# A two-part kernel of local attention and a state-space layer: parameter loads, tables, the layout of C, 128-row blocks and a softmax in two halves

## The chip, the cores and the metric

The kernel runs on one core of a Trainium2 chip. A core has several engines that work side by side, each through its own queue in order: TensorE (PE, with its weight loads shown as PEld), VectorE (DVE), ScalarE (ACT), GpSimd (POOL) and SyncE (SP), which here only issues transfers. An engine's queue that issues transfers is written with a q (SPq, ACTq, POOLq). The metric is the device time of one launch in microseconds (us). PE accumulates into PSUM banks; ACT and DVE copy the results out of them.

## The reference

Two independent layers, each on 2048 tokens of width 448, side by side in the output:

```python
# A: 16 heads of 28; every token attends to itself and 7 tokens at distances 2, 4, ... 14
q, k, v = split_heads(A_x @ A_wqkv)
logits = einsum("bhsd,bhswd->bhsw", q, k[idx]) * 28 ** -0.5      # idx = pos - 2 * arange(8), masked below 0
a = einsum("bhsw,bhswd->bhsd", softmax(logits), v[idx]) -> (2048, 448) @ A_wo
# B: diagonal complex state space, 448 states
Lam_bar = exp(exp(log_dt) * Lam);  B_bar = ((Lam_bar - 1) / Lam)[:, None] * Bmat
Bu = x @ B_bar.T;   h[t] = Lam_bar * h[t-1] + Bu[t]
b = 2 * real(h @ Cmat.T) + x * Dskip
out = concatenate([a, b], -1)                                    # bfloat16
```

## The kernel before

Part A keeps 16 consecutive tokens (j = 0 to 15) in each of 128 partitions. `g_xta` transposes x (xTA) on PE, `proj_j` projects one j (four matmuls of 448 columns) to k_s, q_s or v_s, and `halo` copies the last 14 token slots of a partition to the next partition by four transfers that POOL issues. `qk_unit` makes the logits of one distance w for half of the j (jh = 0 or 1): DVE multiplies q and k (L363), adds the products down from 28 to 7 rows in two steps (L365, L366), `fill` puts other PE work in between, and seven matmuls with the identity (L370) finish the sum, which ACT copies to L (L371). After all 16 units comes one softmax over L (L439 to L453). The attention stage takes four j at a time (jg): for each w DVE makes pv = attn x v (L487), PE transposes and sums pv over w in the banks of acc (L492), ACT copies acc to oT (L496), and `wo_tile` applies wo (L474) later, out of the list of work.

Part B works on chunks of T = 4 tokens: 512 chunks are columns, and 448 complex states are 7 blocks m of 128 rows (64 real, 64 imaginary). The parameters are loaded as 33 rows by twelve small transfers (L72 to L75), transposed by PE (L165) and turned into coefficients on DVE and ACT (L168 to L181); powers of Lam_bar (`s_pow`), gains (`s_gain`) and the matrices R (`s_R`) follow. Cosine and sine tables of 512 steps are made in four pieces q by `s_tab1` to `s_tab4` on ACT and DVE during the k projections, and spread to tab by twelve transfers on SP's queue (L268 to L270). C is laid out by POOL in copies (L126, L127) and transposed and scaled by `c_prep` during the q projections. `b_prep` transposes B to BT; `bu_tile(m, j)` multiplies it with x (L329) and adds R times the state before (L332). x and B have 448 columns, so that the last of four blocks uses 64 rows, 64 to 127 (`blk_rows`). `ssm_chunk_scan` runs the recurrence over the chunks on DVE for half of the blocks (HF), `fix_tile` adds its result to the other tokens (L392, L393), and `c_tile` makes outputs with C (L403) and the skip term (dgD, L407), again with 64 rows in the last block.

The order of all queues is the order of the program (`manual_schedule`). Work for PE waits in the list `work` with a cost in us for each item, and `fill(us)` takes items until that much is used up. Tiles with one tag share one place in memory: nat (the tables) and L do, C's layout (CC), BT and v_s do, and PSUM has four banks "mm" for projections and tiles, two "tp" for transposes, two "lg" for logits; acc later takes the place of the last four.

Of the kernel before, what the change touches and what calls it, by code (L numbers as in the profile page):

```python
# [14 lines left out]
J = 16  # L15
# [13 lines left out]
def kernel(  # L29
# [39 lines left out]
    rows = const.tile([33, 128], BF16, tag="rows")  # L69
    for r0, vec in ((18, B_log_dt), (7, B_Lambda_im), (0, B_Lambda_re)):  # L70
        for hf in range(2):
            nc.scalar.dma_start(rows[r0:r0 + 7, 64 * hf:64 * hf + 64], vec.rearrange("(m i) -> m i", i=64))  # L72
    for r0, vec in ((25, B_log_dt), (14, B_Lambda_im), (29, B_Dskip)):
        nc.scalar.dma_start(rows[r0:r0 + 3, :], vec[0:384].rearrange("(m i) -> m i", i=128))
        nc.scalar.dma_start(rows[r0 + 3:r0 + 4, :], vec[320:448].rearrange("(m i) -> m i", i=128))  # L75
# [17 lines left out]
    CC = keep.tile([128, 12800], BF16, tag="v", name="CC")  # L93
    Cn = CC[:, 0:3584].rearrange("p (k r n) -> p k r n", k=4, r=2)
    Cil = CC[:, 3584:10752].rearrange("p (s k m a i) -> p s k m a i", s=2, k=4, m=NM, a=2)
    nsn = CC[:, 10752:12800].rearrange("p (q c) -> p q c", q=4)
# [4 lines left out]
    nc.sync.dma_start(Bn[0:64], B_B_re.rearrange("(m i) n -> i m n", i=64))  # L101
    nc.sync.dma_start(Bn[64:128], B_B_im.rearrange("(m i) n -> i m n", i=64))
# [6 lines left out]
    load_w(2)  # L109

# [13 lines left out]
    for s_ in range(2):  # L124
        for ri in range(2):
            nc.gpsimd.tensor_copy(Cil[:, s_, 0:3, :, ri ^ s_, :], Cn[:, 0:3, ri].rearrange("p k (m i) -> p k m i", i=64))  # L126
            nc.gpsimd.tensor_copy(Cil[0:64, s_, 3, :, ri ^ s_, :], Cn[0:64, 3, ri].rearrange("p (m i) -> p m i", i=64))  # L127
# [18 lines left out]
    def halo(eng, dst):  # L146
        eng.dma_start(dst[1:65, 0:HALO], dst[0:64, J:JK])
        eng.dma_start(dst[65:113, 0:HALO], dst[64:112, J:JK])
        eng.dma_start(dst[112:128, 0:HALO], dst[111:127, J:JK])
        eng.dma_start(dst[0:1, 0:HALO], dst[0:1, J:JK])  # L150
# [12 lines left out]

    tpp = psum_t.tile([128, 4, 128], BF16, tag="tp", name="tpp")
    PE.transpose(tpp[:, 0, 0:33], rows[:], ident[0:33, 0:33])  # L165
    prm = const.tile([128, 33], F32, tag="prm")
    V.tensor_copy(prm[:], tpp[:, 0, 0:33])
    lre, lim, lima, lda, dsk = prm[:, 0:7], prm[:, 7:14], prm[:, 7:18], prm[:, 18:29], prm[:, 29:33]  # L168
    dt = pt_("dt", 11); ACT.activation(dt[:], lda, ACTF.Exp)
    are = tt(pt_("are"), dt[:, 0:7], lre, ALU.mult)  # L170
    th = tt(pt_("th", 11), dt, lima, ALU.mult)
    r = pt_("r"); ACT.activation(r[:], are[:], ACTF.Exp)
    rT = pt_("rT"); ACT.activation(rT[:], are[:], ACTF.Exp, scale=float(T))
    f = ts(pt_("f"), th[:, 0:7], 1.0 / (2 * PI), ALU.mult)
    fT = ts(pt_("fT", 4), th[:, 7:11], float(T) / (2 * PI), ALU.mult)
# [5 lines left out]
    ACT.activation(cs[:], af1[:], ACTF.Sin, bias=hpib[:], scale=-2 * PI * SHR)  # L181


    nat = keep.tile([128, 2, 4, NC], BF16, tag="L", name="nat")
    pw = const.tile([128, T - 1, 2, NM], F32, tag="pw")
# [4 lines left out]
    tabs = {}  # L190

    def s_tab1(q):
        c1 = slice(q, q + 1)
        yy = early.tile([128, NC], F32, tag="yy", name="yy")
        kM = early.tile([128, NC], F32, tag="kM", name="kM")
        nfr = early.tile([128, NC], F32, tag="nfr", name="nfr")
        tabs[q] = nfr
        ACT.activation(yy[:], iot[:], ACTF.Identity, scale=fT[:, c1])
        V.tensor_scalar(kM[:], iot[:], fT[:, c1], MAGIC, ALU.mult, ALU.add)
        V.scalar_tensor_tensor(nfr[:], kM[:], -MAGIC, yy[:], ALU.add, ALU.subtract)  # L200

    def s_tab2(q):
        ACT.activation(nat[:, 1, q, :], tabs[q][:], ACTF.Sin, scale=-2 * PI * SHR)

    def s_tab3(q):
        afr = early.tile([128, NC], F32, tag="afr", name="afr")
        ACT.activation(afr[:], tabs[q][:], ACTF.Abs)
        tabs[q] = afr

    def s_tab4(q):  # L210
        ACT.activation(nat[:, 0, q, :], tabs[q][:], ACTF.Sin, bias=hpib[:], scale=-2 * PI * SHR)
# [8 lines left out]

    gr = {}
# [20 lines left out]
    dgD = bk.tile([128, 4, 128], BF16, tag="dgD")  # L242

    def s_dgD():
        for blk in range(4):
            V.tensor_scalar(dgD[:, blk, :], ident[:], dsk[:, blk:blk + 1], None, ALU.mult)

    side = {}
    for q in range(4):
        for n, fn in enumerate((s_tab1, s_tab2, s_tab3, s_tab4)):  # L250
            side[4 * q + n] = [(fn, (q,))]
    side[2].append((s_pow, ()))
    side[6].append((s_gain, ()))
    side[10].append((s_dgD, ()))
    for jg in range(4):
        for kt in range(4):
            g_xta(jg, kt)
        for j in range(4 * jg, 4 * jg + 4):
            proj_j(1, k_s, HALO, j)
            for fn, args in side[j]:  # L260
                fn(*args)
    halo(nc.gpsimd, k_s)
    s_R()
    V.tensor_scalar(nsn[:], nat[:, 1], -1.0, None, ALU.mult)

    tab = bk.tile([128, 2, NM, NC], BF16, tag="tab")
    for dst, c, srcs in ((lo, 0, nat[:, 0]), (hi, 0, nat[:, 0]), (lo, 1, nsn), (hi, 1, nat[:, 1])):
        nc.sync.dma_start(tab[dst, c, 0:6:2, :], srcs[lo, 0:3, :])  # L268
        nc.sync.dma_start(tab[dst, c, 1:6:2, :], srcs[hi, 0:3, :])
        nc.sync.dma_start(tab[dst, c, 6, :], srcs[hi, 3, :])  # L270
# [3 lines left out]
    Cw = bk.tile([128, NM, D], BF16, tag="Cw")  # L274

    def c_prep(m):
        tps = []
        for s_ in range(2):
            tp = psum_t.tile([128, 512], BF16, tag="tp", name="tp")
            for dq in range(4):  # L280
                n = 64 if dq == 3 else 128
                PE.transpose(tp[:, 128 * dq:128 * dq + n], Cil[0:n, s_, dq, m].rearrange("p a i -> p (a i)"), ident[0:n, 0:n])
            tps.append(tp)
# [3 lines left out]


    for n, j in enumerate(list(range(8, 16)) + list(range(0, 8))):
        if n < NM:  # L290
            c_prep(n)
        proj_j(0, q_s, 0, j)
    early_ctx.close()
# [8 lines left out]

    BT = keep.tile([128, 4, NM, 128], BF16, tag="v", name="BT")

    def b_prep(m):
# [4 lines left out]
        ACT.copy(BT[:, :, m, :], tp[:])  # L310
    for m in range(NM):
        work.append((0.23, b_prep, (m,)))

    def blk_rows(blk):
        return slice(64, 128) if blk == 3 else slice(0, 128)

    late = {}
    bz = ctx.enter_context(tc.tile_pool(name="b_z", bufs=1, side="right"))

    def new_z():  # L320
        late["Z"] = bz.tile([128, NM, T, NC], BF16, tag="Z", name="Z")
        late["scr"] = bk.tile([128, NM, NC], BF16, tag="scr", name="scr")
    work.append((0, new_z, ()))

    def bu_tile(m, j):
        Z = late["Z"]
        ps = psum.tile([128, 512], F32, tag="mm", name="mm")
        for blk in range(4):
            PE.matmul(ps[:], BT[blk_rows(blk), blk, m, :], xT4[blk_rows(blk), blk, j, :],  # L329
# [4 lines left out]
    HF = (range(0, 4), range(4, 7))  # L334
    for ms in HF:
        for j in range(T):
            for m in ms:
                work.append((0.86 if j == 0 else 1.08, bu_tile, (m, j)))
# [4 lines left out]
    def v_halo():  # L343
        halo(nc.gpsimd, late["v"])

    def new_v():
        late["v"] = keep.tile([128, JK, DH, H], BF16, tag="v", name="v_s")
    work.append((0, new_v, ()))
    for j in range(J):
        work.append((0.76, v_tile, (j,)))  # L350
    work.append((0, v_halo, ()))


    L = keep.tile([128, W, JH], F32, tag="L", name="L")


    UNITS = [(w, 1) for w in range(5)] + [(w, 0) for w in range(5)] + [(w, jh) for w in range(5, 8) for jh in (1, 0)]

    def qk_unit(u, us):
        w, jh = UNITS[u]  # L360
        off = HALO - 2 * w
        pr = qkp.tile([128, DH, JH // 2], BF16, tag="prod", bufs=2, name="prod")
        V.tensor_tensor(pr.rearrange("p d (j h) -> p d j h", h=H), q_s[:, :, 8 * jh:8 * jh + 8, :],  # L363
                        k_s[:, off + 8 * jh:off + 8 * jh + 8].rearrange("p j d h -> p d j h"), ALU.mult)
        V.tensor_tensor(pr[:, 0:14, :], pr[:, 0:14, :], pr[:, 14:28, :], ALU.add)  # L365
        V.tensor_tensor(pr[:, 0:7, :], pr[:, 0:7, :], pr[:, 7:14, :], ALU.add)  # L366
        fill(us)
        lg = psum_l.tile([128, JH // 2], F32, tag="lg", name="lg")
        for d in range(7):
            PE.matmul(lg[:], ident[:], pr[:, d, :], start=(d == 0), stop=(d == 6))  # L370
        ACT.copy(L[:, w, 128 * jh:128 * jh + 128], lg[:])  # L371

    def ssm_chunk_scan(ms):
        Z, scr = late["Z"], late["scr"]
# [14 lines left out]
    def fix_tile(m, j):  # L389
        Z = late["Z"]  # L390
# [7 lines left out]
    def c_tile(j, ct):  # L398
        Z = late["Z"]
# [131 lines left out]
```

## Time and profile before

| | us |
|---|---|
| three runs | 228.36, 226.02, 223.96; median 226.02 |
| profiled execution | 225.31, its span 223.5 |
| PE busy (1376 matmuls) | 178.9 (80%) |
| PE weight loads | 106.2 (48%) |
| DVE busy | 158.1 (71%) |
| ACT busy | 101.3 (45%) |
| POOL busy | 15.1 (7%) |

The stages in the timeline of that execution: the first matmul of k at 13.94, of q at 40.2, the first transposes of B at 61.35, the first matmul of v at 102.65, the last c tile at 156, the first matmul of attention at 168.17, the last copy out of PSUM until 220.5. The span is the time between the first and the last instruction in the profile. In the page a slice is a fortieth of the span, its digit the tenth of it in which the engine was busy; PEclk is the clock granted to TensorE in tenths. In the timeline a line has start, duration, engine, line of the program, operation, tiles, shape and count, and in brackets the idle time before it with what ended it.

### The profile page before, as it was taken

The page shows a single profiled execution, that of the slowest core. Times are in us where ns is not written, and L with a number is a line of the kernel's source. Part 1 is how long each engine was busy: PE and PEld are TensorE (multiplying, and loading weights), DVE is VectorE, ACT ScalarE, POOL GpSimd, SP SyncE. Part 2 cuts the span into 40 slices and gives each one's busy share as a digit, 9 for nine tenths or more (in the row PEclk, how much of TensorE's full clock was granted, in tenths as well). Part 3 has the DMA queues.
Part 4 walks back from the last instruction along what each step waited for, and adds up shares of the span by engine and source line. Part 5 has one row for each costly group of instructions (what it writes and reads, how often), then busy time and mean ns, then how long its engine had stood idle before and what let it go on. Part 6 is the DMA issues. An engine that isn't in the chain of part 4 may idle for free. (4 is left out here: it accounts for less than half of the span.)

```text
span 223.5 us, 3466 instructions
## 1 busy us (share of the span) xinstructions
PE 178.9 (80%) x1376; PEld 106.2 (48%) x1380; DVE 158.1 (71%) x190; ACT 101.3 (45%) x187; POOL 15.1 (7%) x37
## 2 busy tenths in 40 slices
PE   0084679599979999999999799999009979797973
PEld 0052345355534333434544456555009968686851
DVE  0059676833936889799999999987399998584002
ACT  0265178746684445445789723333600022415151
POOL 4039000201000000000010200000000000000000
PEclk9999699979999999999999999999855969999998
DMA  6899970599600000000019421111002001111102
GB/s 189 253 246 185 190 149 19 125 198 186 96 0 0 3 0 0 0 0 3 0 31 191 67 66 62 63 53 62 30 0 76 0 3 43 44 41 43 42 26 97
DMA packets 19911, 16.10 MB, mean 72 GB/s; under 512 B 9624, under 2 KB 19128, under 8 KB 19640
## 3 DMA queue, kind: packets, MB, share of 16 engines
q1 hardware_dynamic: 19372, 12.65, 23.9%
q0 software_dynamic: 416, 3.24, 8.1%
q8 instruction: 10, 0.16, 0.3%
q14 instruction: 5, 0.04, 0.1%
q10 hardware_dynamic: 108, 0.01, 0.0%
HBM read 5.05 MB, written 3.67 MB: 39 GB/s over the span
## 5 line engine op out<-in xcount | busy, mean ns | idle before, releaser
L492 PE MATMUL acc<-ident,pv 128*112 128x128 bf16 x512 | 34.6, 233 | 16.0 <-DVE pv L487 11.6
L492 PEld LDWEIGHTS <-pv 128*112 128x112 bf16 x512 | 34.3, 143 | 18.3 <-DVE pv L487 12.0
L363 DVE TENSOR_TENSOR prod<-q_s,k_s 128x3584 bf16<-128x3584 bf16 x16 | 32.3, 2021 | 9.0 <-PE lg L370 7.8
L487 DVE TENSOR_TENSOR pv<-attn,v_s 128x1792 bf16<-128x1792 bf16 x32 | 32.8, 1085 | 4.6 <-PE acc L492 4.5
L329 PE MATMUL mm<-xT,BT 128*128 128x512 bf16 (+1 forms) x108 | 31.0, 381 | 0.2
L142 PEld LDWEIGHTS <-xTA 112*128 112x128 bf16 x192 | 19.0, 104 | 18.6 <-issue 3.2
L333 ACT CAST Z<-mm 128x512 bf16<-128x512 f32 x28 | 16.4, 586 | 19.9 <-PE mm L332 16.5
L403 PE MATMUL mm<-Cw,Z 128*128 128x448 bf16 x112 | 23.9, 353 | 0.0
L329 PEld LDWEIGHTS <-BT 128*128 128x128 bf16 x112 | 10.0, 97 | 18.0 <-issue 13.0
L479 ACT CAST ya<-mm 128x448 bf16<-128x448 f32 x14 | 7.5, 533 | 22.9 <-PE mm L474 19.9
L365 DVE TENSOR_TENSOR prod<-prod 128x1792 bf16<-128x1792 bf16 x16 | 17.5, 1092 | 0.5
L410 ACT CAST yo<-mm 128x448 bf16<-128x448 f32 x16 | 8.5, 532 | 20.0 <-PE mm L407 20.0
L496 ACT CAST oT<-acc 112x2048 bf16<-112x2048 f32 x4 | 7.5, 1866 | 21.7 <-PE acc L492 21.7
L474 PE MATMUL mm<-wo_p,oT 112*128 112x448 bf16 x64 | 14.9, 364 | 1.2 <-ACT oT L496 1.2
L142 PE MATMUL mm<-wk,xTA 112*128 112x448 bf16 x64 | 15.7, 403 | 0.0
L142 PE MATMUL mm<-wq,xTA 112*128 112x448 bf16 x64 | 14.4, 374 | 0.0
L403 PEld LDWEIGHTS <-Z 128*128 128x128 bf16 x112 | 10.0, 98 | 7.9
L144 ACT CAST k_s<-mm 128x448 bf16<-128x448 f32 x16 | 8.4, 525 | 9.7 <-PE mm L142 9.6
L136 PE MATMUL tp<-ident,xh 128*112 128x128 bf16 x64 | 6.4, 253 | 7.4 <-DVE xTA L137 7.4
L142 PE MATMUL mm<-wv,xTA 112*128 112x448 bf16 x64 | 12.3, 352 | 0.0
L477 DVE CAST ya<-mm 128x448 bf16<-128x448 f32 x2 | 1.2, 624 | 14.9 <-PE mm L474 14.9
L144 ACT CAST q_s<-mm 128x448 bf16<-128x448 f32 x16 | 8.5, 532 | 6.8 <-PE mm L142 6.8
(116 smaller groups left out, 229.5 us busy)
## 6 DMA issues: line engine op xcount, KB each, us to landing
xh<-in_A_x_dram SPq DMA_DIRECT2D x4, 448.0 KB, 3.4
out_dram<-yo SPq DMA_DIRECT2D x16, 112.0 KB, 1.7
out_dram<-ya SPq DMA_DIRECT2D x16, 112.0 KB, 1.7
tab<-nat SPq DMA_DIRECT2D x6, 192.0 KB, 11.5
k_s<-k_s POOLq DMA_DIRECT2D x1, 784.0 KB, 6.0
v_s<-v_s POOLq DMA_DIRECT2D x1, 784.0 KB, 5.9
k_s<-k_s POOLq DMA_DIRECT2D x1, 588.0 KB, 11.1
v_s<-v_s POOLq DMA_DIRECT2D x1, 588.0 KB, 9.3
```

Source lines behind the costliest of these rows:

```text
L142: PE.matmul(ps[:, 0:D], xTA[:, kt, j, :], w_of[t][:, kt, :], start=(kt == 0), stop=(kt == 3))
L144: ACT.copy(o_ap, ps[:, 0:D].rearrange("p (h d) -> p d h", h=H))
L329: PE.matmul(ps[:], BT[blk_rows(blk), blk, m, :], xT4[blk_rows(blk), blk, j, :], start=(blk == 0), stop=(blk == 3 and j == 0))
L333: ACT.copy(Z[:, m, j, :], ps[:])
L363: V.tensor_tensor(pr.rearrange("p d (j h) -> p d j h", h=H), q_s[:, :, 8 * jh:8 * jh + 8, :], k_s[:, off + 8 * jh:off + 8 * jh + 8].rearra ...
L365: V.tensor_tensor(pr[:, 0:14, :], pr[:, 0:14, :], pr[:, 14:28, :], ALU.add)
L403: PE.matmul(ps[:, 0:D], Z[:, m, j, cols], Cw[:, m, :], start=(m == 0), stop=False)
L410: ACT.copy(yo[:], ps[:, 0:D])
L474: PE.matmul(ps[:, 0:D], oT[:, kt, j, :], wo_p[:, kt, :], start=(kt == 0), stop=(kt == 3))
L479: ACT.copy(ya[:], ps[:, 0:D])
L487: V.tensor_tensor(pv[:], attn[:, w, JG * H * jg:JG * H * (jg + 1)].rearrange("p (j h) -> p j h", h=H) .unsqueeze(2).to_broadcast((128, JG, ...
L492: PE.matmul(acc[0:KT, kt, jj, :], pvf[:, jj, KT * kt:KT * (kt + 1)], ident[:], start=(w == 0 and jj == 0), stop=(w == W - 1 and jj == JG - 1))
```

## The change

- The parameters come in four loads, each vector twice side by side (128 columns for 7 blocks); four transposes make the columns, and the forms for 128-row blocks are put together by small DVE copies (`to_blocks`, for dsk and fT).
- PE runs 24 zero matmuls of 128 columns ahead of these transposes and 12 behind them (`idle`).
- The table steps keep their four pieces for the fraction (`s_yy`, `s_frac`), at other places of the k projections, but sin, the absolute value (now on DVE) and cos are each one operation on 2048 elements (`t_sin`, `t_cos`) in the q projections; the spread takes eight transfers, after the second last q projection. `s_R` is queued in the last k projection.
- C is laid out by twelve DVE copies (`c_side`) after the k projections, in three strips (re, im, re) of which `c_prep` takes two neighbours; `c_prep` comes with every second q projection.
- The fourth block of B and of the skip term has 128 rows, whose first 64 weights are zero.
- BT is prepared one m ahead of its bu tile. The units of jh = 1 come first, those of jh = 0 after the scans with one add less and 14 matmuls for the sum. The softmax runs by halves of j (`soft_max`, `soft_norm`), the attention takes jg = 2, 3, 0, 1, copies acc to oT in four pieces and runs wo directly after each jg.
- `halo`'s third transfer begins one partition later.

The diff, cut:

```diff
-    rows = const.tile([33, 128], BF16, tag="rows")
-    for r0, vec in ((18, B_log_dt), (7, B_Lambda_im), (0, B_Lambda_re)):
-        for hf in range(2):
-            nc.scalar.dma_start(rows[r0:r0 + 7, 64 * hf:64 * hf + 64], vec.rearrange("(m i) -> m i", i=64))
...
+    VECS = (B_log_dt, B_Lambda_re, B_Lambda_im, B_Dskip)
+    rows = const.tile([NM, len(VECS), 2, 64], BF16, tag="rows")
+    for n, vec in enumerate(VECS):
+        nc.scalar.dma_start(rows[:, n], vec.rearrange("(m o i) -> m o i", o=1, i=64).to_broadcast((NM, 2, 64)))
...
+    zero = const.tile([128, 128], BF16, tag="zero")
+    V.memset(zero[:], 0.0)
+    idle_ps = psum_l.tile([128, 128], F32, tag="lg", name="idle_ps")
+    def idle(n):
+        for _ in range(n):
+            PE.matmul(idle_ps[:], zero[:], zero[:], start=True, stop=True)
...
-            nc.gpsimd.tensor_copy(Cil[:, s_, 0:3, :, ri ^ s_, :], Cn[:, 0:3, ri].rearrange("p k (m i) -> p k m i", i=64))
-            nc.gpsimd.tensor_copy(Cil[0:64, s_, 3, :, ri ^ s_, :], Cn[0:64, 3, ri].rearrange("p (m i) -> p m i", i=64))
...
-        eng.dma_start(dst[112:128, 0:HALO], dst[111:127, J:JK])
+        eng.dma_start(dst[113:128, 0:HALO], dst[112:127, J:JK])
...
+    def to_blocks(dst, src):
+        V.tensor_copy(dst[lo, 0:4], src[lo, 0:7:2])
+        V.tensor_copy(dst[hi, 0:3], src[hi, 1:6:2])
+        V.tensor_copy(dst[hi, 3:4], src[hi, 6:7])
+    idle(24)
     tpp = psum_t.tile([128, 4, 128], BF16, tag="tp", name="tpp")
-    PE.transpose(tpp[:, 0, 0:33], rows[:], ident[0:33, 0:33])
+    for n in range(4):
+        PE.transpose(tpp[:, 0, 8 * n:8 * n + NM], rows[:, n].rearrange("m a i -> m (a i)"), ident[0:NM, 0:NM])
+    idle(12)
...
+    side = {2: [(s_pow, ())], 5: [(s_yy, (0,))], 6: [(s_gain, ()), (s_frac, (0,))], 8: [(s_yy, (1,))],
+            10: [(s_frac, (1,)), (s_dgD, ())], 11: [(s_yy, (2,))], 13: [(s_frac, (2,))], 14: [(s_yy, (3,))],
+            15: [(s_frac, (3,)), (s_R, ())]}
...
+    def c_side(k):
+        for s_, ri in enumerate((0, 1, 0)):
+            n = 64 if k == 3 else 128
+            V.tensor_copy(Cil[0:n, k, :, s_, :], Cn[0:n, k, ri].rearrange("p (m i) -> p m i", i=64))
+    c_side(0); c_side(1); c_side(2); c_side(3)
...
+    def t_sin():
+        ACT.activation(nat[:, 1], nfr[:], ACTF.Sin, scale=-2 * PI * SHR)
+        V.scalar_tensor_tensor(afr[:], nfr[:], -1.0, nfr[:], ALU.mult, ALU.max)
+    def t_cos():
+        ACT.activation(nat[:, 0], afr[:], ACTF.Sin, bias=hpib[:], scale=-2 * PI * SHR)
+        V.tensor_scalar(nsn[:], nat[:, 1], -1.0, None, ALU.mult)
+        for dst, c, srcs in ((lo, 1, nsn), (hi, 1, nat[:, 1]), (lo, 0, nat[:, 0]), (hi, 0, nat[:, 0])):
+            nc.sync.dma_start(tab[dst, c, 0:7:2, :], srcs[lo, 0:4, :])
+            nc.sync.dma_start(tab[dst, c, 1:6:2, :], srcs[hi, 0:3, :])
     for n, j in enumerate(list(range(8, 16)) + list(range(0, 8))):
-        if n < NM:
-            c_prep(n)
+        if n == 1:
+            t_sin()
+        if n % 2 == 1 and n < 14:
+            c_prep(n // 2)
         proj_j(0, q_s, 0, j)
+        if n == 14:
+            t_cos()
...
+    nc.gpsimd.memset(BT[lo, 3], 0.0)
...
-            PE.matmul(ps[:], BT[blk_rows(blk), blk, m, :], xT4[blk_rows(blk), blk, j, :],
+            PE.matmul(ps[:], BT[:, blk, m, :], xT4[:, blk, j, :],
...
+    bu = [[(0.86 if j == 0 else 1.08, bu_tile, (m, j)) for j in range(T) for m in ms] for ms in HF]
+    fix = [[(0.43, fix_tile, (m, j)) for j in range(T - 1) for m in ms] for ms in HF]
+    work += bu[0]
+    for w in range(4):
+        qk_unit(w, 1, 3.0, True)
+    fill(99)
+    work += bu[1]
+    for w in range(4, 6):
+        qk_unit(w, 1, 3.0, True)
     ssm_chunk_scan(HF[0])
+    fill(99)
     ssm_chunk_scan(HF[1])
+    late["v"] = keep.tile([128, JK, DH, H], BF16, tag="v", name="v_s")
+    work += [(0.76, v_tile, (j,)) for j in range(J)] + fix[0]
     fill(99)
+    halo(nc.gpsimd, late["v"])
+    work += fix[1][:6]
+    fill(99)
+    work += fix[1][6:] + [(1.55, c_tile, (j, ct)) for j in [T - 1] + list(range(T - 1)) for ct in range(4)]
+    qk_unit(6, 1, 1.5, True)
+    qk_unit(7, 1, 2.5, True)
+    soft_max(1)
+    qk_unit(0, 0, 2.5, False)
+    qk_unit(1, 0, 2.5, False)
+    soft_norm(1)
+    fill(3.0)
+    for w in range(2, 8):
+        qk_unit(w, 0, 2.3, False)
+    soft_max(0)
+    fill(99)
...
+    for jg in (2, 3, 0, 1):
...
+            if jg == 2 and w == 4:
+                soft_norm(0)
...
+        for jj in range(JG):
+            j = JG * jg + jj
+            if jg == 1 and jj % 2 == 1:
+                V.tensor_copy(oT[:, :, j, :], acc[0:KT, :, jj, :])
+            else:
+                ACT.copy(oT[:, :, j, :], acc[0:KT, :, jj, :])
+        for jj in range(JG):
+            wo_tile(JG * jg + jj, jg == 1)
```

`soft_max(jh)` masks with POOL, takes the maximum over w, subtracts it (DVE) and exponentiates (ACT) for 128 of the 256 columns of L; `soft_norm(jh)` adds up, inverts and multiplies to attn (DVE).

## The prediction, made before the result was known

> **What bounds the kernel now.** I read the page first: its slices of busy time and granted clock show which stage has which limit.
>
> ```profile
> span 223.5 us, 3466 instructions
> PE   0084679599979999999999799999009979797973
> DVE  0059676833936889799999999987399998584002
> PEclk9999699979999999999999999999855969999998
> ```
>
> A slice is 5.6 us. TensorE (PE) idles in slices 1 and 2, limps through 3 to 11, is full from 12 to 27, idles in 28 and 29 with the clock falling, then works on to the end. DVE is nearly full from 16 to 27 too, so in the middle two engines are close to binding at once. Next I read the timeline of the first 45 us.
>
> ```profile
> 7.61 0.26 ACTq L75 DMA_DIRECT2D rows<-in_B_Dskip_dram  x1
> 11.20 0.18 PE L165 MATMUL tpp<-ident,rows 33*128 33x33 bf16 x1 [11.20 <-DMA rows<-in_B_Dskip_dram]
> 13.94 4.78 PE L142 MATMUL mm<-wk,xTA 112*128 112x448 bf16 x16
> 18.76 3.49 DVE L156 TENSOR_TENSOR pw<-pw 128x7 f32<-128x7 f32 x1
> 20.93 1.30 POOL L126 COPY CC<-CC 128x1344 bf16<-128x1344 bf16 x1
> 24.36 1.01 PE L136 MATMUL tp<-ident,xh 128*112 128x128 bf16 x8 [5.19 <-DVE xTA L137]
> 36.25 3.32 PE L142 MATMUL mm<-wk,xTA 112*128 112x448 bf16 x16
> 39.73 2.96 DVE L239 TENSOR_TENSOR R<-II,cf 128x2688 bf16<-128x2688 bf16 x1
> ```
>
> Three readings. PE's queue starts with the transpose of the parameters, so everything waits for the twelfth small load (issued 7.61, there at 11.2), while x and wk have long landed. A DVE operation on 7 numbers takes 3.49 us while POOL lays out C (its neighbours take 0.16): DVE is held, the xTA copies behind it are late, and PE waits 5.19. Sixteen projection matmuls need 4.78 us at 14 us and 3.32 at 36; their weight loads stand 0.37 apart at first and 0.19 later, a half and a full clock. The timeline around 92 us shows one tile of the B stage.
>
> ```profile
> 91.33 0.39 PE L332 MATMUL mm<-Z,R 128*128 128x512 bf16 x1
> 91.56 1.13 PE L329 MATMUL mm<-xT,BT 128*128 128x512 bf16 x4
> 92.30 0.09 PEld L329 LDWEIGHTS <-BT 64*128 64x128 bf16 x1 [0.42 <-issue]
> 92.62 0.39 PE L332 MATMUL mm<-Z,R 128*128 128x512 bf16 x1
> ```
>
> From R matmul to R matmul are 1.29 us for five matmuls of 0.215: the 64-row weights are loaded late and cost 0.21. Last, the softmax.
>
> ```profile
> 164.63 2.29 DVE L453 TENSOR_TENSOR attn<-L,m 128x2048 bf16<-128x2048 f32 x1
> 168.17 10.19 PE L492 MATMUL acc<-ident,pv 128*112 128x128 bf16 x128 [11.64 <-DVE pv L487]
> 178.40 1.87 ACT L496 CAST oT<-acc 112x2048 bf16<-112x2048 f32 x1 [18.04 <-PE acc L492]
> ```
>
> PE does nothing for 11.64 us, then also waits for each of four 1.87 us copies. The chain of waits is the softmax, then the attention stage on PE to the end.
>
> **To the first k matmul (13.94 before).** Four loads replace twelve. The first six were issued by 3.1, the seventh only at 4.65, so the eight removed carry the lateness. Landing takes 3.4 us for an xh load and 5.1 for wk; four loads issued by 2.4 should be there between 4.2 and 6.3, I take 5.3. Four transposes take 0.4. DVE then has the old chain (11.42 to 12.66, 1.24 us) and six block copies of 0.16, less the 0.28 in which it waits for ACT anyway: 1.9 us ahead of the xTA copies. From the first of these to the first matmul are 1.28 (12.66 to 13.94): k starts at 8.9. The zero matmuls: 0.37 x 128/448 = 0.107 each at half clock; 24 end by 3.9, before the loads; 12 take 1.3, under DVE's 1.9. So they cost nothing; without that cover, 1.3. wk is there at 6.3. **-5.0 us.**
>
> At best the zero matmuls make k start warm. The trace went to full speed at 17.2, after 3.3 us of unbroken work; 24 of them are 2.6 us. I take half clock for the first part of k, 1.1 us, between 0 (warm) and 2.9 (16 x 0.18).
>
> [...]
>
> **k stage (13.94 to 39.6 before).** A warm group of four j is 4.61 us (31.64 to 36.25), 3.05 of it matmuls. Without POOL's copies the 5.19 stall goes, and with it the half clock at 24.3 to 27.4. What is late next is DVE's side work: powers 14 x 0.17 = 2.4, gain 1.9 + fraction 1.2 = 3.1, fraction + dgD 2.0, each against 3.05 of matmuls. Hidden, within 0.2. 3.05 + 3 x 4.61 + 1.1 = 18: k ends at 26.9. **-7.7 us.** The twelve ACT table steps of 512 leave this stage; ACT had room.
>
> **q stage (39.6 to 61.35 before): the loss.** The C layout moves into DVE's queue, behind the last fraction (waits for ACT's yy; done 1.3 after k ends), R (0.55 + 2.96) and ahead of all Cw. Twelve copies of 448 bf16: no such row. Below, DVE's smallest operation, 0.16; above, the xTA copy (512 from PSUM), 0.42. I take 0.25, nearer the small end since the 2048-element bf16 negation takes only 0.69: 3.0 us, between 1.9 and 5.0. PE transposes for c_prep(0) after one projection, and needs all twelve: it stands from 0.75 to 7.8 after k. Then afr (2048, four times 0.69 = 2.8) is ahead of the first Cw, and c_prep(1) waits 0.6 for that. PE's work: 16 x 0.755 + 7 x 0.95 = 18.7. Sum 18.7 + 7.05 + 0.6 = 26.3. After so long an idle time the clock halves, as at 44.4 to 47.9 (granted 0.51): 1.5. 27.8 against 21.75: **+6.0 us**; q ends at 54.7, called T.
>
> [...]
>
> **T to the first attention matmul (106.8 before).** PE's entry is later: on ACT the one cos (2048; as the exp of 2048, 1.91) stands ahead of the last q copy and of BT's copies, so the first bu tile starts at T+2.9. POOL's zeros for BT (896 elements; twice the 0.56 copy of 448) are under that.
> - bu: 7 x 4 x 0.215 + 21 x 5 x 0.215 = 28.6, where 34.5 stood (-5.9). If 128 rows don't cure the gap, 0.
> - preps 1.4, six logit groups of seven at 0.4, v 16 x 0.755: to T+47.5.
> - 21 fix tiles at ACT's pace 0.495 (the 18 copies in 8.91), three c tiles 7 x 0.19 + 4 x 0.056 = 1.55 each (before 1.73), two logit groups: to T+63.4. DVE has finished its eight products and both scans (14.6 + 11.3) by T+56 and waits.
> - The softmax's operations have half the columns. The trace has them whole: 1.23, 0.69, 0.43, 2.29 for the maximum and the difference, the reciprocal 1.75; a half costs about the next smaller one (128 elements: 0.29, between 0.16 for 7 and 0.43 for 256). L copy and POOL's memset 0.65, maximum 0.69 + 0.43 + 0.29 + 1.23 + gaps = 2.75; its exp is under the products. DVE: two products with one add (2.02 + 1.09 = 3.15), normalization (0.69 + 0.43 + 0.29 + 0.9 + 1.23 + gaps) 3.65, six products 18.9: with stalls of 0.1 on PE T+95.8. PE has 14-matmul groups of 0.8 and the last thirteen c tiles; it waits 3.5 for the first of these products and 2 to 4 at the end, when c tiles have run out. Then group 0.8, copy and memset 0.7, maximum 2.75, pv 1.09: T+101.2.
> Clock lost in these two waits: 1.0. 102.2 against 106.8: **-4.6 us.**
>
> L takes the slot of nat, and the table transfers (eight instead of twelve, the same bytes) now start only at T-0.2, behind the last cos; SP's queue holds nothing else until the first output. 1.79 MB at about 0.2 MB/us (53 to 55 us) land at T+10; L's first copy wants T+7.8. ACT stands still, but PE has four mm buffers, 4 us of tiles. Cost 0; every us past T+11.5 is on the path.
>
> **Attention to the end (55.3 before).** First group: seven pv 7.6, normalization of the other half 3.65 in DVE's queue, last matmuls 0.95: 12.2. This group is of the j whose logits came first, so that only one half of the softmax stands ahead of it. Then three times oT piece 0.6 + four wo 3.04 + 128 x 0.0565 = 10.87 (before 11.54), and 0.6 + 3.04 + ya 0.62 + 3.0 from the last copy to the end. 52.1: **-3.2 us.** wo_p's load is free to go before this stage. The halo's third piece no longer waits 10.9 for the second: nobody needed it.
>
> **Sum.** -5.0 - 7.7 + 6.0 - 4.6 - 3.2 = -14.5. The profiled execution had 225.3 (span 223.5); the median shown is 226.0. 225.3 - 14.5 = 210.8: **211 us.**
>
> **Rivals.**
> - *Slower: L's slot.* In the trace the same table transfers took from 37.3 to past 57, with single issues of 3.28 and landings of 11.5. Eight such issues and one landing end at T+37.5: ACT's first L copy holds all behind it for 26 us: 237. It decides against the change from T+26. Against: the slow ones ran beside k_s's halo, which is over by then.
> - *128 rows cure nothing.* 28 x 0.21 + 16 x 0.18 = 8.8 come back: 220. Against: matmuls with full rows stand 0.215 apart.
> - *The q stall is short.* Copies at 0.16 and a clock that stays up, k warm: 1.1 + 1.1 + 1.5 + 1.0 less: 206.
> - *The clock stays down* through k's start (1.8 more), twice as long after the q stall (1.5) and in the first attention group (16 x 0.107 = 1.7 per pv instead of 1.09 for the last three, 1.9): 216.
>
> **How the numbers follow.** Forecast (208 to 214) 0.48; shorter stall 0.16; clock 0.16; no cure 0.08; L's slot 0.06; nothing of these, another wait of 10 us or more, 0.06. Range 203 to 221. About 2% (221.5 and 230.5) is what a measurement of this kernel can tell from no change: faster 0.86, same 0.07, slower 0.07.
>
> **What would show it.** Right: tpp near 5.5; no 3.49 us power; PE idle about 7 us before the first Cil transpose; bu tiles of 1.08; an attention start with 4 us of idle in front. Wrong: ACT idle ahead of its first L copy with PE following; bu tiles still at 1.29; more than 10 us of PE idle in q.

## The result, and the profile after

The changed kernel takes 212.62 us (median of four runs, 210.73 to 212.74); the kernel before, beside it, 227.19 (223.96 to 228.39). The ratio is 0.943, with a 95% interval of 0.931 to 0.955. The profiled execution took 212.74, its span is 211.0. Forecast were 211 and a range of 203 to 221. Ratios, here and below, leave out executions that were over 1.5% slower than the fastest of their kernel.

The page of the changed kernel first, with slices of 5.3 us:

```profile
span 211.0 us, 3648 instructions
PE   5699952999789999999999949999428589898983
DVE  0569769613695998999996099998959999988013
PEclk9999996599979999999999999999955999999999
```

TensorE works from slice 1 on. Three holes are left: slices 5 and 6 (the q stage; the clock falls in 6 and 7), slice 23 (the first product behind the first half of the softmax) and 28 to 31 (the last logits and the wait ahead of the attention, the clock falling in 29 and 30). PEclk shows no half clock in the first slices; that k starts at half clock is read from the distances of its weight loads, 0.37 and then 0.19, as in the prediction. DVE's row has a hole in slice 22, where before it was nearly full. The timeline of the first 40 us:

```profile
4.91 0.18 PE L175 MATMUL tpp<-ident,rows 7*128 7x7 bf16 x1 [1.05 <-DMA rows<-in_B_Lambda_re_dram]
7.05 0.18 PE L175 MATMUL tpp<-ident,rows 7*128 7x7 bf16 x1 [0.52 <-DMA rows<-in_B_Dskip_dram]
10.61 4.09 PE L144 MATMUL mm<-wk,xTA 112*128 112x448 bf16 x16
15.99 3.32 PE L144 MATMUL mm<-wk,xTA 112*128 112x448 bf16 x16
33.23 3.59 DVE L270 COPY CB<-CB 128x448 bf16<-128x448 bf16 x12
33.96 0.29 PE L279 MATMUL tp<-ident,CB 128*128 128x128 bf16 x1 [4.52 <-DVE CB L270]
34.84 0.29 PE L279 MATMUL tp<-ident,CB 128*128 128x128 bf16 x1 [0.59 <-DVE CB L270]
36.74 2.27 DVE L290 SCALAR_TENSOR_TENSOR afr<-nfr 128x2048 f32<-128x2048 f32 x1
```

The last three parameter loads are there at 4.91, 6.34 and 7.05, one after another; the first is there by 3.67, when PE has finished its 24 zero matmuls (at 2.14 in e2, which has none). The k stage has no stall (the 3.49 us power and the 5.19 us wait are gone). In q, PE stands for 4.52 us and then three times for 0.59 behind DVE's copies of C. Two windows of the same stage (columns: stretch, its length, then busy time and count of PE, PEld, DVE, ACT and POOL, the granted clock, the DMA share, GB/s):

```profile
34.00:36.00 2.00, 0.82 (x3) 0.26 (x3) 2.00 (x8) 0.00 (x0) 0.00 (x0) 0.50 1.35 257
40.00:42.00 2.00, 2.00 (x12) 1.04 (x11) 0.28 (x1) 1.12 (x2) 0.00 (x0) 0.50 0.01 1
```

The clock is still 0.50 after the stall, when PE has no gap. By the windows around these it is a half from 32.9 to 43.15. The timeline of the B stage and of the end:

```profile
67.03 0.27 ACT L407 COPY L<-lg 128x128 f32<-128x128 f32 x1 [1.30 <-PE mm L349]
...
73.28 0.38 PE L349 MATMUL mm<-Z,R 128*128 128x512 bf16 x1
73.50 1.03 PE L346 MATMUL mm<-xT,BT 128*128 128x512 bf16 x4
74.36 0.38 PE L349 MATMUL mm<-Z,R 128*128 128x512 bf16 x1
...
121.05 0.69 DVE L420 TENSOR_TENSOR m<-L 128x512 f32<-128x512 f32 x1 [6.80 <-POOL L L417]
...
126.91 0.95 PE L406 MATMUL lg<-prod,ident 128*128 128x128 bf16 x14 [3.37 <-DVE prod L398]
...
158.83 6.46 PE L505 MATMUL acc<-ident,pv 128*112 128x128 bf16 x80 [4.38 <-DVE pv L498]
...
170.62 2.04 ACT L512 CAST oT<-acc 112x512 bf16<-112x512 f32 x4 [11.70 <-PE acc L505]
```

bu tiles are 1.08 apart (1.29 before). ACT waits 1.30 us ahead of its first L copy, and no PE row of this stretch shows a wait for it. DVE has nothing to do for 6.80 us ahead of the first half's softmax, and PE then waits 3.37 for the first product behind it (predicted 3.5). PE waits 4.38 ahead of the attention, 11.64 before, and then four copies of a quarter of acc take 2.04 us together.

### The profile page after: what moved, and what is told of

Same layout as the page of the kernel before. It is cut to its first block, busy times and chain, and to the rows that moved or that the text cites. A ratio compares the mean times of both kernels' runs of the same rounds, so it can differ in the third digit from the quotient of the medians.

```text
span 211.0 us, 3648 instructions
## 1 busy us (share of the span) xinstructions
PE 177.9 (84%) x1471; PEld 113.2 (54%) x1475; DVE 156.8 (74%) x214; ACT 99.1 (47%) x195; POOL 9.1 (4%) x33
## 3 DMA queue, kind: packets, MB, share of 16 engines
HBM read 5.05 MB, written 3.67 MB: 41 GB/s over the span
## 4 chain that ended last, share of the span: by engine, by line
PE 56%; DVE 10%; issue 3%; ACT 2%; POOL 0%; POOLq 0%; DVEq 0%
PE mm L346 12%; PE acc L505 12%; PE mm L382 8%; PE mm L485 6%; PE mm L144 6%; PE lg L406 4%; DVE pv L498 3%; PE mm L372 2%; PE mm L373 2%; PE mm L349 2%; DVE prod L396 2%; PE mm L385 1%; DVE L L423 1%; ACT oT L512 1%; DVE prod L398 1%
## 5 line engine op out<-in xcount | busy, mean ns | idle before, releaser
L505 PE MATMUL acc<-ident,pv 128*112 128x128 bf16 x512 | 31.5, 226 | 6.6 <-DVE pv L498 6.6
L505 PEld LDWEIGHTS <-pv 128*112 128x112 bf16 x512 | 31.1, 136 | 7.5 <-DVE pv L498 7.0
L346 PE MATMUL mm<-xT,BT 128*128 128x512 bf16 x108 | 29.7, 396 | 2.5 <-ACT BT L335 2.3
L512 ACT CAST oT<-acc 112x512 bf16<-112x512 f32 x14 | 7.3, 595 | 32.2 <-PE acc L505 31.5
L406 PE MATMUL lg<-prod,ident 128*128 128x128 bf16 x168 | 12.7, 227 | 6.4 <-DVE prod L398 6.4
L346 PEld LDWEIGHTS <-BT 128*128 128x128 bf16 x112 | 10.6, 101 | 13.6 <-ACT BT L335 3.2
L406 PEld LDWEIGHTS <-ident 128*128 128x128 bf16 x168 | 10.8, 102 | 8.3 <-DVE prod L398 6.9
L485 PE MATMUL mm<-wo_p,oT 112*128 112x448 bf16 x64 | 12.8, 353 | 2.7 <-ACT oT L512 2.7
L144 PE MATMUL mm<-wk,xTA 112*128 112x448 bf16 x64 | 14.0, 370 | 0.0
L283 DVE SCALAR_TENSOR_TENSOR Cw<-tp,be,ctmp 128x448 bf16<-128x448 bf16 x7 | 4.8, 682 | 11.4 <-ACT ctmp L282 11.4
L279 PE MATMUL tp<-ident,CB 128*128 128x128 bf16 (+1 forms) x56 | 7.3, 235 | 6.3 <-DVE CB L270 6.3
```

The lines of the kernel that those rows point to most:

```text
L144: PE.matmul(ps[:, 0:D], xTA[:, kt, j, :], w_of[t][:, kt, :], start=(kt == 0), stop=(kt == 3))
L346: PE.matmul(ps[:], BT[:, blk, m, :], xT4[:, blk, j, :], start=(blk == 0), stop=(blk == 3 and j == 0))
L485: PE.matmul(ps[:, 0:D], oT[:, kt, j, :], wo_p[:, kt, :], start=(kt == 0), stop=(kt == 3))
L505: PE.matmul(acc[0:KT, kt, jj, :], pvf[:, jj, KT * kt:KT * (kt + 1)], ident[:], start=(w == 0 and jj == 0), stop=(w == W - 1 and jj == JG - 1))
L512: ACT.copy(oT[:, :, j, :], acc[0:KT, :, jj, :])
```

## The experiments

Each kernel is the changed one with one edit, unless said otherwise. The kernel before, run beside them, had medians of 226.4 to 228.0. T is the first transpose of B; a stage lasts from its first matmul to that of the next.

Stages of one profile each were comparable here only to within 1 to 2 us, as half-clock stretches came and went in stages whose code is the same. The q code of the changed kernel took 27.7 (e5), 27.4 (e6), 27.5 (e8), 26.9 (e2), 26.5 (e10) and 26.4 us (e1); by the windows, 10.2 us of the 27.7 in the first profile are at half clock, and 6.9 of the 26.5 in e10. T to the first v matmul took 36.9 or 37.0 where half clock falls among the first bu tiles (3.4 us by the windows of the changed kernel; in e2, e5, e6 and e8 the longest transpose of B, 0.31 us, shows it) and 35.4 where it does not (e3, no transpose of B over 0.22; e10, by its PE rows; e12, granted 1.00 from 56 to 64).

**64 rows again (e1).**

```diff
-            PE.matmul(ps[:], BT[:, blk, m, :], xT4[:, blk, j, :],
+            PE.matmul(ps[:], BT[blk_rows(blk), blk, m, :], xT4[blk_rows(blk), blk, j, :],
```

(and the same for the skip term in `c_tile`)

> The changed kernel with the 64-row fourth block back in the B stage and in the skip term (the zero weights stay in memory, unread). Theory (a 64-row block makes PE load its weights late, 0.21 us for each tile): state tiles go from 1.08 back to 1.29, output tiles from 1.55 to 1.73; 28 x 0.21 + 16 x 0.18 = 8.8 us longer, 221. Rival (DVE binds in the middle, PE only shares it): the B tiles are hidden and 2 to 3 us come back, 215. Rival (row count is without effect, the gap went with the new order): 212.6.

220.6 us, ratio 0.965 (0.958 to 0.972), span 218.9. The timeline of its B stage has the old distance, 1.29 from one R matmul to the next:

```profile
77.23 0.39 PE L352 MATMUL mm<-Z,R 128*128 128x512 bf16 x1
77.46 1.13 PE L349 MATMUL mm<-xT,BT 128*128 128x512 bf16 x3
78.52 0.39 PE L352 MATMUL mm<-Z,R 128*128 128x512 bf16 x1
```

The rows are worth 7.9 us of span in this kernel. From T to the first v matmul it takes 40.8 us instead of 36.9, from the first c tile to the attention 49.0 instead of 44.0. This split holds some clock: e1's first bu tiles ran at full clock (granted 1.00 from 57 to 77; against 35.4 the difference is 5.4, near the 5.9 expected), but its c stage has a half-clock stretch that the changed kernel's does not have: from 118 to 130 the clock is granted at 0.97, and single c matmuls take up to 0.58 us, against 0.35 at most in the changed kernel.

**128 rows alone, in the kernel before (e9).** The same edit the other way round, with zeros in the first 64 weights.

> The kernel before with one part of the change alone: the fourth block of B and of the skip term has 128 rows, of which the first 64 weights are zero; parameters, tables, C layout, order of units and softmax stay as before. Theory (the price is TensorE's, 0.21 us for each of 28 bu tiles and 0.18 for each of 16 c tiles, wherever they stand): -5.9 to -8.8 us, 217 to 220 where the kernel before has 226 (ratio 0.96 to 0.975); bu tiles 1.08 apart. Rival (in the kernel before, DVE is nearly full in the middle too, so that TensorE gains and then waits for the products and for the softmax): less than 3 us, ratio above 0.985, with a longer TensorE wait ahead of the attention (11.6 before).

224.36 us, ratio 0.993 (0.987 to 1.000): the rival is right about the total. The bu tiles are 1.08 apart here too, yet from T to the attention it takes 104.7 us instead of 106.8. DVE's products and scans follow each other without a gap from 80 us on (19.56 of 20 us busy in 80 to 100), and PE now waits for DVE's scan, which it did not before:

```profile
123.16 0.38 PE L396 MATMUL mm<-Z,R 128*128 128x511 bf16 x1 [1.86 <-DVE Z L390]
```

The time to T is 4.0 us longer than in the kernel before and the attention 3.1 shorter. In q the clock was at a half for 13.6 us here and for 3.4 there, though PE has hardly a gap after 44.8; in the attention the windows have it at a half for some 6.5 us less here. The edit does no work in q or in the attention beyond two memsets, and why the clock differs there was not tried; these two numbers are not counted for or against the rows. What is shown: 128 rows alone save 2.1 us in the stage that they are meant for; e9 has a half-clock stretch among its first bu tiles (some 70.4 to 73.8 by its PE rows; granted 0.91 over 60 to 80) that the kernel before does not have (1.00 over 56 to 76), so it may be up to 1.5 more. The 7.9 need something of the rest of the change. That it is the changed order (one add less on DVE for half the units, and these units after both scans), which gave DVE time, is argued from DVE's rows; no run has the order alone.

**No zero matmuls (e2), and only the 12 (e6).**

```diff
-    idle(24)
...
-    idle(12)      # kept in e6
```

> The changed kernel without the 36 zero matmuls. Theory (24 end at 3.74, long before the last parameter load at 7.05, the clock is at half all the same when k starts, and the 12 lie under DVE's parameter chain): same within 1 us, first k matmul at 10.6, clock open near 12.4. Rival (they bring the clock up earlier): k's first sixteen matmuls take 6.0 instead of 4.1, 214.5. Rival (the 12 hold up the first transposes): 1.2 us shorter.

> The changed kernel with the 12 zero matmuls behind the parameters' transposes and without the 24 ahead of them. Without all 36 the clock opened at 15.6 instead of 12.4 and k's end came 1.6 us later. Theory (the 12 fill the last cold window, the 24 end long before it): as the changed kernel, clock open at 12 to 13, span 211. Rival (the 24 matter too, as activity is added up from the start): clock open near 15.6, span 213. [...]

Without any, 214.89 us, ratio 0.941 (0.936 to 0.946), span 213.1; with the 12, 212.71, ratio 0.947 (0.942 to 0.952), span 210.9. The ratios' intervals overlap (the two ran on different chips); the spans and the first 16 projections of k (timelines of e2, then of e6) tell them apart:

```profile
10.62 5.65 PE L144 MATMUL mm<-wk,xTA 112*128 112x448 bf16 x16
```

```profile
10.51 3.51 PE L144 MATMUL mm<-wk,xTA 112*128 112x448 bf16 x16
```

k starts at the same time, but by the weight loads the clock opens at 15.6 without zero matmuls and at 12.4 with all; with the 12 it is at about 11, an estimate from 3.51 against 3.30 in the warm start of e8. My "no effect" fell, and the rival of an earlier clock (214.5) was right. The k stage takes 19.5 us without zero matmuls and 17.9 with all: 1.6. The size is uncertain, as with all 36 in the same place the first 16 projections took from 3.31 (e12) over 4.09 (the changed kernel) to 4.66 us (e10):

```profile
10.70 4.66 PE L144 MATMUL mm<-wk,xTA 112*128 112x448 bf16 x16
```

That is 1.0 to 2.3 less than 5.65. The 12 between the parameters' transposes and k do it: e6's 3.51 lies within that spread. The 24 before them add nothing that can be seen in this place, where PE then waits for loads.

**Parameters first (e8).** The four small loads go ahead of x on SyncE's queue.

```diff
-        nc.scalar.dma_start(rows[:, n], vec...)
+        nc.sync.dma_start(rows[:, n], vec...)
```

> The changed kernel with the four parameter loads issued by SP ahead of x and the weights instead of by ACT beside them. In the changed kernel they came at 3.7, 4.9, 6.3 and 7.05. Theory (a small load waits in the transfer engines behind the large ones that were issued before): all four there by 4.5, x 1.4 later, first k matmul at 8.0 to 8.5 instead of 10.6, span 208.5 to 209. Rival (a load of 128-byte pieces for seven partitions takes 1.2 us by itself, one after the other): last one at 6.5 or later, first k matmul unchanged within 0.5, span 211. Rival (x and wk come 1.4 later and take the place of the parameters): first k matmul 9.5 to 10.5.

209.08 us, ratio 0.930 (0.916 to 0.943), span 207.7. Timeline:

```profile
3.68 0.26 PE L175 MATMUL tpp<-ident,rows 7*128 7x7 bf16 x4
...
5.93 0.65 PE L138 MATMUL tp<-ident,xh 128*112 128x128 bf16 x8 [0.92 <-DMA xh<-in_A_x_dram]
...
7.45 3.30 PE L144 MATMUL mm<-wk,xTA 112*128 112x448 bf16 x16
```

All four are there at 3.68. Issued beside the large loads, on ScalarE's queue, they were there only at 7.05. The edit changes the queue together with the order, and no run has one alone. For the order speak the issues on ScalarE's queue: the load issued with the first large one, at 0.74, was there after 1.4 us, the next, issued at 1.36 behind it, after 3.1 to 3.6 (timelines of e2, which has no zero matmuls ahead of these transposes, and of the changed kernel above):

```profile
2.14 0.18 PE L174 MATMUL tpp<-ident,rows 7*128 7x7 bf16 x1 [2.14 <-DMA rows<-in_B_log_dt_dram]
4.45 0.18 PE L174 MATMUL tpp<-ident,rows 7*128 7x7 bf16 x1 [2.13 <-DMA rows<-in_B_Lambda_re_dram]
```

k starts 3.2 us earlier, and warm: the first 16 projections take 3.30.

**C laid out by POOL again (e3).** Six copies (three strips) on POOL ahead of the k stage, none on DVE.

```diff
+        nc.gpsimd.tensor_copy(Cil[:, 0:3, :, s_, :], Cn[:, 0:3, ri].rearrange(...))
...
-    c_side(0); c_side(1); c_side(2); c_side(3)
```

> The changed kernel with the layout of C on POOL again (six copies, three strips, queued at the place of before), c_prep as changed. Theory (POOL's copies hold DVE, DVE's copies hold PE): the k stage grows by 3 to 5 us through late xTA copies, and the q stage loses its 4.5 us of standing, 3 us of waits between copies and the half clock, 8 in all: 207 to 210, so that laying out C on DVE at that place is a loss. Rival (POOL's copies cost DVE nothing and before was slow there for another reason): 204.5. Rival (moving the layout to DVE is a gain, as the k stage's 7.8 us come from it): 215 or more.

212.35 us, ratio 0.930 (0.925 to 0.935), span 209.9. The gain is 1.1 us of span, not 3 to 6. DVE's small operations are late beside POOL's copies in k again (1.65 us for one on 7 numbers, where its neighbours take 0.15 to 0.17), and in q there still are R and afr ahead of the first Cw:

```profile
16.56 1.65 DVE L166 TENSOR_SCALAR nr<-pw 128x7 f32<-128x7 f32 x1
22.01 0.71 PE L142 MATMUL tp<-ident,xh 128*112 128x128 bf16 x8 [2.23 <-DVE xTA L143]
39.52 0.46 PE L282 MATMUL tp<-ident,CB 128*128 128x128 bf16 x4 [3.31 <-DVE Cw L286]
```

k takes 3.6 us more than in the changed kernel, q 4.1 less, and the start and the later stages make up the rest of the 1.1. So moving the layout from POOL to one lump of DVE work ahead of q neither gains nor loses much; that taking C from POOL pays when it is spread, the next run shows. The second rival fell too: POOL's copies (six, where the kernel before has eight) bring back 3.6 of the 7.7 us by which k had become shorter, not all.

**C's copies spread over k (e4), and the tables early too (e7).**

```diff
+            10: [(s_frac, (1,)), (c_side, (0,)), (c_side, (1,))], 11: [(s_yy, (2,))],
+            13: [(s_frac, (2,)), (c_side, (2,))], 14: [(c_side, (3,)), (s_yy, (3,))], 15: [(s_frac, (3,))]}
...
+        if n == 3:
+            t_sin()
         proj_j(0, q_s, 0, j)
+        if n == 8:       # e7; e4 has it at 14, behind s_R and s_dgD
+            t_cos()
         if n == 14:
+            s_R()
+            s_dgD()
```

> The changed kernel with C's twelve DVE copies queued in the last two groups of k (where DVE has room), and R and dgD made after the last Cw. Theory (PE's standing in q is the queue order on DVE, and the half clock follows from it): q from 27.7 to 19.5, k at most 0.5 longer: 204.5. Rival (DVE has no room in k, xTA copies come 0.9 late three times): 207. Rival (the middle is bound by DVE, which gets nothing earlier): 209 or more.

> The kernel with C's copies spread over k and R after the last Cw, with the cos and the eight table transfers moved up from behind q projection 14 to behind projection 8. In the spread kernel the q stage was 10 us shorter, but ACT's first copy to L stood 5.9 us for the table transfers out of the place that L takes, and the first B tile 2.1 us for ACT's cos. Theory (these two gave the gain back): q end near 48, first v matmul 34 to 35 us after q's end instead of 41, 5 to 7 us shorter than the spread kernel: span 201 to 203. Rival (DVE's chain of products and scans binds the middle from the start, and PE's earlier tiles wait for it): 1 to 3 us shorter, 205 to 206. Rival (the cos in the middle of q holds ACT, PE waits for the four banks there): q 2 us longer, 204.

e4: 209.92 us, ratio 0.921 (0.916 to 0.926), span 207.6. q takes 18.0 us instead of 27.7 and k 0.9 more, but from T to v it takes 41.1 instead of 36.9, by the wait that the prediction's rival of L's slot named, at another size:

```profile
62.79 0.27 ACT L409 COPY L<-lg 128x128 f32<-128x128 f32 x1 [5.88 <-DMA tab<-nat]
63.59 1.87 PE L348 MATMUL mm<-xT,BT 128*128 128x512 bf16 x4 [2.58 <-ACT Z L352]
```

T comes 9 us earlier and cos does not: ACT stands 5.88 us ahead of the L copy until the table transfers are out of L's place, and PE 2.58 behind it. e4's total is the one that its last rival named (209 or more, a middle bound by DVE), but for another reason: with cos six projections earlier (e7) both waits go, at 205.68 us, ratio 0.915 (0.909 to 0.921), span 203.9, and T to v in 35.7. That is 3.7 of span less than e4 where I expected 5 to 7: T to v is 5.5 shorter, but q is 1.2 and k 0.4 longer, and R and dgD still stand ahead of DVE's first product, for which PE waits 1.42.

**Zero matmuls in the q stall (e12).**

```diff
         if n == 1:
             t_sin()
+            idle(80)
...
+                if m == 0 and s_ == 0 and dq < 3:
+                    idle(12)      # behind the first transposes of C
```

> The changed kernel with 116 more zero matmuls in TensorE's stall of the q stage: 80 behind the first q projection, 12 behind each of the first three transposes of C; their result is used by nothing. In the changed kernel TensorE has nothing for 4.52 us there, and the clock is granted at 0.50 from 32.91 to 43.15; from 37.35 on it works without a gap, 5.8 us of work at half speed. Theory (the clock follows TensorE's idle time, and the q stage's loss holds some 3 us of clock beside the stall itself; the prediction had 1.5): the half-clock window in q goes, q takes 24.5 to 25.5 instead of 27.7, span 208 to 209, total 209.5 to 210.5. Rival 1 (DVE's copies, afr and Cw set the pace of q, not the clock): the clock stays up and q takes 27 or more. Rival 2 (zero matmuls don't keep the clock, as two dozen did nothing ahead of the parameters): the window stays, and q is 0 to 1 us longer.

209.21 us, ratio 0.933 (0.921 to 0.945), span 207.5. q takes 25.5 instead of 27.7, with the same DVE work at the same distances; the windows have the clock at 1.00 from 26 to 54. The same two stretches as above:

```profile
34.00:36.00 2.00, 2.00 (x31) 1.67 (x30) 2.00 (x8) 0.03 (x1) 0.00 (x0) 1.00 1.07 209
40.00:42.00 2.00, 2.00 (x16) 1.16 (x15) 0.21 (x1) 1.60 (x3) 0.00 (x0) 1.00 0.01 1
```

So the clock's part in q is 2.3 us against this profile of the changed kernel (1.1 by e10, whose half-clock stretch in q is shorter, 6.9 us, and 0.9 by e1), and the stall's own is about 6.3 (4.52 and three times 0.59). The other 1.2 us of span are not shown to be the zero matmuls' doing: k started warm in this profile (0.8 less), the c tiles to the attention took 1.1 more, and in the first bu tiles the clock was full, where the changed kernel had it at a half from 60.2 to 63.6, so that T to v took 35.4 instead of 36.9; but e10 and e3 have the same 35.4 without zero matmuls in q.

**C tiles held back for the softmax (e10).**

```diff
-    fill(3.0)
     for w in range(2, 8):
-        qk_unit(w, 0, 2.3, False)
+        qk_unit(w, 0, 1.5, False)
```

> The changed kernel, but the c tiles are spread thinner over the late logit units (1.5 us of fill for each instead of 2.3, and no 3.0 ahead of them), so that three are left for the second softmax half. Theory (TensorE's 2 us ahead of the last logits and most of its 4.4 ahead of the attention stand with the clock falling to a half): the half-clock window ahead of and in the attention's first group goes away, 1 to 2 us less than the changed kernel, 210.5 to 211.5 (span 209 to 210). Rival (DVE's products and the softmax set the time, and the tiles only move inside a wait): the attention starts at the same time, within 0.5 us, and the total is the same.

212.51 us, ratio 0.945 (0.936 to 0.955): the same as the changed kernel. In its profile, the attention starts at 155.36 instead of 158.83; 2.1 of these 3.5 us come from the stages before the c tiles, 1.4 from the tiles. From there to the end it takes 53.4 instead of 52.2, so 1.3 of the 1.4 are given back (53.44 less 52.17): a window in the first attention group shows DVE busy all the time with pv, PE half of it.

```profile
162.00:166.00 4.00, 2.09 (x20) 2.09 (x21) 4.00 (x5) 0.00 (x0) 0.00 (x0) 0.73 0.11 29
```

What PE loses ahead of the attention (4.38 us and the clock) is hidden behind DVE's pv.

**The changed kernel again (e5),** beside e6, e7 and e8 on one chip:

> The changed kernel once more, as the measure for the other three on this chip: ratio to before 0.93 to 0.95, span 209 to 211.

212.49 us, ratio 0.945 (0.937 to 0.953); each stage starts within 0.2 us of the first profile's time.

**All mended (e11).** e7 with e8's loads and e10's tiles, R behind the tenth q projection, dgD behind the second scan.

> The changed kernel with what the runs so far point to, in one: the four parameter loads first on SyncE's queue, the C layout in the last two groups of k, sine at the fourth and cosine after the ninth q projection, R after the tenth instead of behind the last but one, dgD behind the second scan, c tiles held back for the second softmax half. Theory (the terms are of different stages and add up): 205.7 of the kernel with early tables, less 3.2 for the loads, less 1 to 1.5 for R and dgD off the first product, less 1 to 2 for the c tiles: 199 to 201 (span 197 to 199), first k matmul near 7.4, T near 45, first product not waited for. Rival (DVE is then the bound in the B stage and gives it back there): 203 or more, with v's first matmul over 37 us after T.

201.19 us, ratio 0.895 (0.886 to 0.903), span 199.1: better than both kernels, and 0.2 us above the range that I expected. T came at 46.7, not near 45. Against the changed kernel's profile: k starts 2.8 earlier (7.84); k 18.0, the same; q 20.9, 6.8 less; T to attention 98.1, 4.5 less; the end 54.3, 2.1 more. The sum, -12.0, is the difference of the spans (11.9) but for rounding. The first product no longer waits (DVE is at 45.35, before T). Two prices remain: R now stands ahead of a Cw in q (PE waits 1.68 us), and the attention is longer, where DVE's pv set the pace in e10. In the B stage DVE gave nothing back: T to v takes 33.8, the rival wanted over 37.

## Why the prediction was right

The total was 1.6 us off, the profiled execution 1.9. Of the signs that the prediction named, three came (no 3.49 us power, bu tiles of 1.08, some 4 us of idle time ahead of the attention) and two did not: the parameters' transposes ended at 7.05 and not near 5.5, and PE stood 4.52 us ahead of the first transpose of C, not 7. By stages:

| stage | before | predicted | measured |
|---|---|---|---|
| first k matmul at | 13.94 | 8.9 | 10.61 |
| k stage | 25.6 | 18.0 | 17.9 |
| q stage | 21.75 | 27.8 | 27.7 |
| T to first attention matmul | 106.8 | 102.2 | 102.6 |
| from there to the end of the span | 55.3 | 52.1 | 52.2 |

In the column of before, k ends with its last matmul (39.6), as transposes of C come ahead of the first matmul of q.

**The mis-sized term** is the landing of the parameters: I took 5.3 for all four, between 4.2 and 6.3 by the landings of two large loads, and the last came at 7.05, outside of these bounds. In the first k matmul that is 1.7 of the 1.9 us missing; DVE's chain behind it took 2.05 (predicted 1.9). e8 shows that four loads can be there by 3.68, so that their number is not the cause; order and queue, which e8 changes together, are. Two large loads had given me the duration; for four small ones issued beside them it was no measure.

**Wrong, and hidden by the sum.** "They cost nothing" was right of the zero matmuls, and half clock for the first part of k as well (16 projections in 4.09 us; I had 3.05 and 1.1). But without them it would have been 5.65: the kernel without zero matmuls was not the one that I had costed, and what they bring (some 1.6 us) was in my sum without being named. I had set the 24 alone (2.6 us) against the 3.3 us of work after which k came to full speed in the kernel before, and left the 12 out. e6 shows that the 12 count, which the transposes of x follow (3.51 for the same 16), and in e8, where all 36 run from 1.00 to 5.01 with hardly a break, k is warm from its start (3.30).

The q stage came out at 27.7 from other parts than mine: copies of C 0.30 each, not 0.25; a stall of 6.3 instead of 7.05, since PE can transpose a block when that block's three copies are there and not only when all twelve are; the 0.6 behind afr under work at half clock; and 2.3 of clock instead of 1.5 (e12). That these add up to within 0.1 us is luck, the more so as the same q code took 26.4 to 27.7 us from run to run.

**Right, and shown.** The 0.21 us are the price of 64-row weights (e1, with 7.9 us back of 8.8), though e9 says that they count so much only with the rest of the change. L's place in memory costs nothing: the last transfer was issued at 61.09 and such transfers took 5.1 to 5.7 us, so they were out at T+10 to T+10.6 (predicted T+10). ACT's wait of 1.30 ends at T+10.8; its row names a matmul of L349, which the copy of logits does not need, so that it was the transfers is inferred. It was near the limit: e4 goes over it and pays. The first attention group takes 11.8 (12.2), the next ones 11.03 (10.87).

**Right in number, and not shown by a run.** No run takes back the softmax in halves, the quarter copies of acc or the merged table steps, so the terms for the end of the middle stage and for the attention stand on the stage times and on PE's waits alone (4.38 ahead of the attention, 0.68 for each copy to oT). In the k stage I put nearly all of the 7.7 us down to POOL's copies; e3, where PE waits 2.23 for them and not 5.19, brings back 3.6, and the other 4.1 are not shown by a run.

**The rivals.** "128 rows cure nothing" fell with e1. "L's slot" as a loss of 26 us fell; as a mechanism it is in e4 with 4 us. "The q stall is short" fell, "the clock stays down" was half true: in the changed kernel's profile it cost 2.3 us in q (e12) and 1.5 in the first bu tiles (against e10), 3.8 where 1.5 was counted, but in other runs of the same code some 1.0 in q (e10, e1) and nothing in the bu tiles.

## What to carry to other kernels

Read which engine has slack in the stage before crediting a saving: the same 0.21 us per tile were 7.9 us in the changed kernel and 2.1, perhaps up to 3.6, in the kernel before, whose DVE had no gap left in that stage once PE was faster (19.56 of 20 us busy in e9). And before reading 1 or 2 us out of two profiles, look whether their half-clock stretches lie in the same places (the same q code took 26.4 to 27.7 us here). Try the small loads that start everything ahead of the large ones, on one queue (all four there at 3.68 instead of 7.05 in e8), and a side job spread over a stage with slack rather than in one lump ahead of its consumer (q 9.7 us shorter for 0.9 more in k, in e4). And when a stall goes, look for what was hidden under it: here the table transfers that kept L's place (5.88 us of ACT) appeared only when q got short.

## What was not expected of the hardware

**The half-clock stretches came in one length and its multiples.** Those that I worked out from windows are multiples of 3.41 us, to within some 0.05: 3.41 (60.2 to 63.6), 10.24 (32.9 to 43.15, and 152.4 to 162.6), 13.6 (43.1 to 56.8 in e9). In e9's q stage PE's records are without a gap from 44.8 on, and the clock was granted at a half until 56.8, 12 us later. Two windows of e9:

```profile
48.00:50.00 2.00, 2.00 (x11) 0.92 (x9) 0.38 (x1) 0.77 (x2) 0.00 (x0) 0.50 1.06 179
50.00:52.00 2.00, 2.00 (x10) 0.95 (x8) 0.68 (x1) 0.42 (x2) 0.00 (x0) 0.50 0.86 139
```

What ends such a stretch is not shown by these rows. In the changed kernel's q stall zero matmuls kept the clock up: with them it is granted at 1.00 from 26 to 54 (e12), without them at 0.50 from 32.9 to 43.15.

**The last of four small loads was there 3.4 us later when they were issued beside large ones** (at 7.05, against 3.68 or sooner in e8, where they go first and also have the other queue), and they then arrived one by one: in e2 at 2.14, 4.45, 6.02 and 7.07.
